# An RWKV-5 and mixture-of-experts kernel on one core: gate weights loaded as rows and turned on TensorE, with five smaller edits of order

## The chip, the cores and the metric

The kernel runs on one core of one Trainium2 chip. The metric is the device time of one execution in microseconds (us). Three runs of the kernel before gave a median of 400.97 us, between 399.18 and 401.94.

The engines are named as the profile names them: PE is TensorE (PEld its weight loads), DVE is VectorE, ACT is ScalarE, POOL is GpSimd, SP is SyncE, which here issues most DMAs.

## The reference

Two parts follow each other. The first is a linear recurrence per head with a decay `w` and a bonus `u`; the second sends each token to one of 16 experts. All numbers are fp32.

```python
# r, k, v: (4, 8, 768, 48); w, u: (8, 48)
for t in range(768):
    cur = k[t] outer v[t], each row times u
    y[t] = r[t] @ (state + cur)
    state = w * state + k[t] outer v[t]
x = y as (3072, 384)                   # tokens by (head, 48)
# experts: w_group (384, 4), w_expert (4, 384, 4), w1 (4, 4, 384, 1024), w2 (4, 4, 1024, 384)
g = argmax(x @ w_group)                # one group for each token
e = argmax(x @ w_expert[g])            # one expert in the group
gate = softmax(x @ w_group)[g] * softmax(x @ w_expert[g])[e]
out = gate * (relu(x @ w1[g, e]) @ w2[g, e])
```

## The kernel before, in words

The order of the work on every engine is written out by hand: each engine runs its instructions in the order in which the code issues them, and semaphores tie the engines together where a tile is shared.

**The recurrence.** The 3072 tokens are 24 tiles `n` of 128, four batches beside each other. One step `s` of the loop at L860 treats one tile. In a step, `values(s)` (L583) multiplies the masked scores `am` with `v` into `y_ps` in bank YB; `values_out(s)` (L612, ACT) copies the result to `yT`; `scores` (L536) makes the scores of a coming tile in bank PA, and `mask` (L543, DVE) writes those below the diagonal into `am`. On the diagonal stands the bonus term: POOL multiplies r, k and u (`own`, L489 and L490), DVE sums it (`sum_own`, L498), DVE writes five of the eight diagonals (`diagonal_here`, L554) and ACT the other three (`diagonal`, L561; they are kept in `waiting` and issued behind the next `values_out`). `update` (L594) makes the new part of the state in `u_ps`, in bank MS, which `carry` (L604, or L607 and L608 from tile 4 on, DVE) adds to the state R; `state` (L574) applies R. `turn` (L511) transposes k and r of a tile that comes later into the banks TR and RW; ACT copies k out (L520), DVE multiplies r by the powers of w on its way out (L522). POOL's `scaled` (L493) prepares k in the ring `kp`.

Up to `CLOSE = 5` a step makes the scores of tile s+1, and from then on those of tile s+2; step 4 turns one tile more than the others. Ahead of the loop, tiles 0 and 1 are prepared by the same helpers. Empty transposes of the identity (`turn_nothing`, L422) run in four places there: 13 at the start, 2, then 2 and 4.

**Routing.** `gate_parts(n)` (L619) multiplies yT with the gates' weights `gwp`, four quarters at once, into a bank (MS or TR, by the tile's number), and ACT copies the parts to `lT` (L624). `gate_sum` (L644) adds the quarters into the logits LG, also in MS. `rows_out` (L630, L634) turns y into rows of tokens. For four tiles at once the `route_` helpers on DVE find expert, gate and place; `route_5` (L230, POOL) scatters the rows of tokens to `x_sorted`, a DRAM tensor with a region for each expert. Four `fill` DMAs (L439) write zeros there first, in the steps 5 to 8.

`gwp` is filled by five DMAs (`gates_in`, L406 and L409), issued on SP behind the loads of the first three pairs of tiles. They read the weights in pieces of four numbers, since a partition of `gwp` holds one of a head's 48 dimensions. `gates_twice` (L412, POOL) copies a part of them to the partitions from 64 on.

In step 0 DVE compares w with its limited copy (`out_of_range`, L752), and PE and DVE make one flag of it (L756, L759); it decides at the very end whether a slow exact path runs.

**Experts.** From L1016 on the experts run one after another in the order of their numbers of tokens. Each has SLOTS[s] places for tokens; the two with most tokens are also computed ahead for 128 tokens each. `up` (L1104) and `down` (L1116) are the two products, `finish` transposes the result back and scatters it in pieces (L1128, POOL). The last to run is slot 0 with 96 places. Its `down` is done by `rows_down` (L240): tokens lie on the partitions of the result, ACT multiplies by the gate (L244), and one indirect DMA writes rows of 384 numbers (L245). `tokens` makes the row numbers `idA` for that.

Of the kernel before, what the change touches and what calls it, by code (L numbers as in the profile page):

```python
# [17 lines left out]
P = 128  # L18
# [11 lines left out]
def kernel(  # L30
# [89 lines left out]
    idA = [cst([P, 1], f"idA_{i}", I32) for i in range(4)]  # L120
    okA = [cst([P, 1], f"okA_{i}", I32) for i in range(4)]
# [130 lines left out]
    def tokens(i, n, count):  # L252
        nc.vector.memset(idA[i][0:n], NOWHERE)
        nc.vector.tensor_scalar(
            out=tagA[i][0:n, 0:1].bitcast(I32), in0=tagA[i][0:n, 0:1].bitcast(I32), scalar1=2, scalar2=None,
            op0=OP.logical_shift_right,
        )
        nc.vector.tensor_scalar(out=okA[i][0:n], in0=prow[0:n], scalar1=count[0:n], scalar2=None, op0=OP.is_lt)
        nc.vector.copy_predicated(idA[i][0:n], okA[i][0:n], tagA[i][0:n, 0:1].bitcast(I32))
# [14 lines left out]
    with ExitStack() as rec:  # L274
# [4 lines left out]
        lT_at = (MS[:, 0:P], TR[:, 0, :])  # L279

# [23 lines left out]
        cnt_ps = MS[:, 464 : 464 + GE]  # L304

# [25 lines left out]
        raw = {}  # L331
        wcol = ring.tile([P, HC], FP32, name="wcol")
# [17 lines left out]
        raw[0, "v"] = load(v, 0, "vt", 4)  # L350
        raw[1, "k"] = load(k, 1, "kt", 3)
# [52 lines left out]
        def gates_in():  # L404
            wg = moe_w_group.rearrange("(h d) g -> d h g", d=D)
            nc.sync.dma_start(out=gwp[0:D, :, 0:G], in_=wg)  # L406
            for g in range(G):
                we = moe_w_expert[g].rearrange("(h d) x -> d h x", d=D)
                nc.sync.dma_start(out=gwp[0:D, :, G + Eg * g : G + Eg * (g + 1)], in_=we)  # L409
# [10 lines left out]
        def turn_nothing(times, bank=RW):  # L420
            for i in range(times):
                nc.tensor.transpose(bank[:, 0, :], ident, ident)  # L422

        turn_nothing(13)
        nc.tensor.matmul(u_ps_all, lhsT=ones[0:1, :], rhs=u_row, start=True, stop=True, skip_group_check=True)
        turn_nothing(2)
        gates_in()
        pads(kp, 0)
        nc.scalar.copy(ub.rearrange("p h d -> p (h d)"), u_ps_all)
        for n in (1, 2, 3):  # L430
            if n < NRP - 1:
                pads(rp, n)
            pads(kp, n)
# [90 lines left out]
        def scores(n):  # L524
            kT, rT = rkT.pop((n, "kT")), rkT[n, "rT"]
            for hc in range(HC):
                for e in range(2):
                    rows = slice(DP * e, DP * e + D)
                    if n == 0:
                        nc.tensor.matmul(  # L530
                            PA[:, e, P * hc : P * (hc + 1)], lhsT=kT[rows, hc, :], rhs=rT[rows, hc, :],
                            start=True, stop=True, skip_group_check=True,
                        )
                        continue
# [79 lines left out]
        def gate_parts(n):  # L614
            yT = yTs[n]
            lT_ps = lT_at[n % 2 if n < 7 else 1]
            for q in range(NQ):
                e, j = q // 2, q % 2
                nc.tensor.matmul(  # L619
                    lT_ps[32 * q : 32 * (q + 1), :], lhsT=gwp[:, 4 * j + e, :], rhs=yT[:, e, j, :],  # L620
                    start=True, stop=True, skip_group_check=True,
                )
            lT = mid[n] = pool.tile([P, P], FP32, tag="lT", bufs=3, name="lT")
            nc.scalar.copy(lT, lT_ps)  # L624
# [60 lines left out]
        def count(n):  # L685
            nc.tensor.matmul(cnt_ps, lhsT=ones, rhs=cum[:, n, :], start=True, stop=True, skip_group_check=True)

# [63 lines left out]
        def out_of_range():  # L751
            nc.vector.tensor_tensor(out=same, in0=wcol, in1=wraw, op=OP.not_equal)  # L752
            nc.vector.reduce_max(out=same[:, 0:1], in_=same, axis=AX)

        def all_out_of_range():
            nc.tensor.matmul(cnt_ps[:, 0:1], lhsT=ones, rhs=same[:, 0:1], start=True, stop=True, skip_group_check=True)  # L756

        def in_range():
            nc.vector.tensor_scalar(out=not_ok, in0=cnt_ps[:, 0:1], scalar1=0.5, scalar2=None, op0=OP.is_gt)  # L759
# [68 lines left out]
        nc.vector.tensor_mul(WL, pw[:, :, P // 2], pw[:, :, P // 2])  # L828
        nc.scalar.copy(wl, WL)
# [3 lines left out]
        turn_nothing(2)  # L833
        turn(1, "rT")
        turn_nothing(4, TR)
        turn(1, "kT")
        scaled(1, 0)
# [22 lines left out]
        for s in range(NT):  # L860
# [11 lines left out]
            del left[0:some]  # L872
            if s == 2:
                gates_twice()
                late_consts()
# [19 lines left out]
            if s in (5, 6, 7, 8):  # L895
                fill(s - 5)
# [10 lines left out]
            values_out(s)  # L907
            if s == 0:
                own_term(1)
                out_of_range()  # L910
            for n, e, hc in waiting:
                diagonal(n, e, hc, hc + 1)
            waiting.clear()
            if s <= CLOSE:
# [13 lines left out]
            if s == 0:  # L928
                all_out_of_range()
                in_range()  # L930
# [11 lines left out]
            for n in {4: (0, 1), 5: (2, 3), 6: (4,), 7: (5, 6)}.get(s, (s - 1,) if s > 7 else ()):  # L942
                gate_sum(n)
            for c in range(NB - 1):
                if s == first(c) + 2:
                    route_p(c)
                    if c == 2:
                        count(12)
            for n in {3: (0, 1), 4: (2, 3), 5: (4,), 6: (5, 6)}.get(s, (s,) if s > 6 else ()):
                gate_parts(n)  # L950
            if s < CLOSE:
                own_term(far)
            for c in range(NB - 1):
# [4 lines left out]
                if s == first(c) + 2:  # L958
                    if c == 2:
                        key = keys()  # L960
                    route_3(c)
# [17 lines left out]
            if s + 1 < NT:  # L979
                state(s + 1)  # L980
            if s == CLOSE - 1:
                turn(s + 3, "kT")
# [6 lines left out]
            if s == 8:  # L989
# [450 lines left out]
```

## Time and profile before

| | us |
|---|---|
| median of three runs | 400.97 |
| profiled execution | 402.09 |
| its span in the profile | 400.3 |
| PE busy in the span | 388.7 |
| ACT / POOL / DVE busy | 180.4 / 201.0 / 153.4 |
| step 0's first values (L583) begin | 12.14 |
| PE's last matmul (L240) ends | 393.14 |

The profile is of one execution. A busy time counts an engine's instructions, not how full each of them uses it. A wait is named by what released it, as far as semaphores show; where the named engine had long been done, something else ended the wait. Times in the timeline count from the start of the span. Entries of the timeline merge like instructions in a row: start, length, engine, line, operation, tiles, count, and in brackets how long the engine was idle before and what ended that.

### The profile page before, as it was taken

To read this page: it belongs to the slowest core of one execution; us is meant where nothing else is said; L and a number is where in the kernel's file an instruction comes from. 1 tells how busy PE (TensorE), PEld (TensorE's weight loads), DVE (VectorE), ACT (ScalarE), POOL (GpSimd) and SP (SyncE) were. 2 spreads that over 40 slices of the span, in tenths; PEclk is the share of its full clock that TensorE was granted. 3 is DMA by queue.
4 is the path that set the end of the run, shared out by engine and by line. 5 is a ranking of instruction groups with operands and counts; after the bars stand their busy time and mean duration, and the time that the engine had idled before them with its cause. 6 is when DMAs were issued, how large, how long until landed. Compare 5 with 4: busy or idle time off the path is not lost.

```text
span 400.3 us, 10467 instructions
## 1 busy us (share of the span) xinstructions
PE 388.7 (97%) x3963; PEld 361.9 (90%) x3963; DVE 153.4 (38%) x405; ACT 180.4 (45%) x429; POOL 201.0 (50%) x265
## 2 busy tenths in 40 slices
PE   8999999999999999999999999999999999999992
PEld 6787899999888977899999999999999999999981
DVE  7887988888867602101202112111121221211110
ACT  4665888888875211432433424424244244244210
POOL 7999956999842412105162351532624524523542
PEclk9999999999999999999999999999999999999999
DMA  8998999995965977999999999999989999981000
GB/s 159 160 174 159 197 208 221 212 195 147 264 200 123 308 193 212 233 275 258 232 258 243 228 250 266 224 253 284 200 240 259 255 247 268 233 236 28 27 18 27
DMA packets 123118, 81.80 MB, mean 204 GB/s; under 512 B 96863, under 2 KB 114289, under 8 KB 123061
## 3 DMA queue, kind: packets, MB, share of 16 engines
q1 hardware_dynamic: 116019, 71.12, 77.1%
q0 software_dynamic: 4752, 9.55, 8.1%
q8 instruction: 32, 0.52, 0.6%
q10 hardware_dynamic: 2290, 0.40, 0.5%
q14 instruction: 25, 0.20, 0.2%
HBM read 69.89 MB, written 11.67 MB: 204 GB/s over the span
## 4 chain that ended last, share of the span: by engine, by line
issue 46%; PE 29%; POOL 18%; SPq 3%; DVE 2%; DMA 1%; POOLq 1%; ACT 0%
POOL out_dram L1128 16%; PE YB L583 6%; PE PA L536 6%; SPq L323 3%; PE TR L511 3%; PE YB L574 2%; PE YB L630 2%; PE RW L511 2%; PE MS L594 2%; PE TR L619 2%; PE MS L644 1%; DMA vt<-in_v_dram 1%; POOL out_dram L245 1%; PE TR L793 1%; DVE am L543 1%
## 5 line engine op out<-in xcount | busy, mean ns | idle before, releaser
L1128 POOL DMA_INDIRECT out_dram<-yt,idn x93 | 90.4, 972 | 137.1 <-DVE yt L1126 107.0
L1076 DVE STREAM_TRANSPOSE xe<-xg 128x672 f32<-128x672 f32 (+2 forms) x16 | 12.7, 796 | 121.0 <-DMA xg<-x_sorted 88.7
L1116 PE MATMUL YB<-hT,w2p 128*128 128x208 f32 (+10 forms) x336 | 58.7, 328 | 0.0
L1116 PE MATMUL PA<-hT,w2p 128*128 128x208 f32 (+10 forms) x336 | 58.1, 326 | 0.0
L1116 PEld LDWEIGHTS YB<-hT,w2p 128*128 128x128 f32 x336 | 55.8, 190 | 0.0
L1116 PEld LDWEIGHTS PA<-hT,w2p 128*128 128x128 f32 x336 | 55.3, 190 | 0.0
L561 ACT ACTIVATE am<-ident,du 128x128 f32<-128x128 f32 x152 | 50.5, 398 | 0.0
L1125 DVE STREAM_TRANSPOSE yt<-yT 128x672 f32<-128x672 f32 (+1 forms) x14 | 11.8, 842 | 80.4 <-ACT yT L1119 80.4
L1094 ACT COPY w2p<-w 128x1024 f32<-128x1024 f32 x42 | 41.1, 1045 | 3.0 <-DMA w<-in_moe_w_dram 3.0
L543 DVE COPY_PREDICATED am<-later,PA 128x1024 f32<-128x1024 int32 x24 | 31.7, 1323 | 10.8 <-PE PA L536 6.1
L1104 PE MATMUL MS<-xe,w 128*128 128x208 f32 (+12 forms) x192 | 32.8, 320 | 0.0
L1104 PE MATMUL TR<-xe,w 128*128 128x208 f32 (+12 forms) x192 | 32.8, 320 | 0.0
L1104 PE MATMUL RW<-xe,w 128*128 128x208 f32 (+12 forms) x192 | 32.8, 320 | 0.0
L1104 PE MATMUL SB<-xe,w 128*128 128x208 f32 (+12 forms) x192 | 32.7, 320 | 0.0
L1104 PEld LDWEIGHTS SB<-xe,w 128*128 128x128 f32 x192 | 30.8, 190 | 0.6 <-issue 0.2
L1104 PEld LDWEIGHTS MS<-xe,w 128*128 128x128 f32 x192 | 30.7, 190 | 0.0
L1104 PEld LDWEIGHTS RW<-xe,w 128*128 128x128 f32 x192 | 30.7, 190 | 0.0
L1104 PEld LDWEIGHTS TR<-xe,w 128*128 128x128 f32 x192 | 30.7, 190 | 0.0
L230 POOL DMA_INDIRECT x_sorted<-xt,place_i x16 | 16.1, 1003 | 23.6 <-DVE end L719 11.8
L536 PE MATMUL PA<-rT,kT 48*64 48x128 f32 (+1 forms) x736 | 25.6, 255 | 0.5 <-issue 0.5
L583 PE MATMUL YB<-am,vt 128*48 128x128 f32 x384 | 25.9, 277 | 0.1
L490 POOL TENSOR_TENSOR dg<-dg,ub 128x384 f32<-128x384 f32 x24 | 24.1, 1003 | 1.9
(220 smaller groups left out, 560.1 us busy)
## 6 DMA issues: line engine op xcount, KB each, us to landing
w<-in_moe_w_dram SPq DMA_DIRECT2D x128, 384.0 KB, 9.5
vt<-in_v_dram SPq DMA_DIRECT2D x24, 192.0 KB, 4.5
rp<-in_r_dram SPq DMA_DIRECT2D x23, 192.0 KB, 4.3
kt<-in_k_dram SPq DMA_DIRECT2D x22, 192.0 KB, 5.2
xg<-x_sorted SPq DMA_DIRECT2D x36, 85.8 KB, 10.3
x_sorted<-zeros SPq DMA_DIRECT2D x4, 392.0 KB, 4.7
out_dram<-yt,idn POOLq DMA_INDIRECT x93, 7.5
xg<-x_sorted SPq DMA_DIRECT2D x20, 73.5 KB, 8.9
```

Source lines behind the costliest of these rows:

```text
L230: ins = nc.gpsimd.indirect_dma_start(out=xs_dram, out_offset=bass.IndirectOffsetOnAxis(ap=place_i[:, i : i + 1], axis=0), in_=xt[:, i].rea ...
L490: nc.gpsimd.tensor_mul(dg, dg, ub)
L511: nc.tensor.transpose(ps[:, hc, :], two, ident)
L536: nc.tensor.matmul(PA[64 * z : 64 * (z + 1), e, P * hc + 64 * z : P * (hc + 1)], lhsT=kT[rows, hc, 64 * z : 64 * (z + 1)], rhs=rT[rows, hc ...
L543: nc.vector.copy_predicated(am[n % NAM], later.unsqueeze(1).unsqueeze(1).to_broadcast([P, 2, HC, P]).bitcast(I32), PA.rearrange("p e (h t) ...
L561: nc.scalar.mul(am[n % NAM][:, e, hc, :], ident, dus[n][:, i : i + 1])
L583: nc.tensor.matmul(y_at(e, hc), lhsT=vt[:, n % 2, 2 * hc + e, :], rhs=amn[:, e, hc, :], start=(n < 4 and hc < 2), stop=True, skip_group_ch ...
L1076: nc.vector.transpose(xe[:, :, 0:nb, :], xg[:, 0:nb, 0:QW].rearrange("p i (ko a) -> p ko i a", a=32))
L1094: nc.scalar.copy(o4[:, kk], v4[:, kk])
L1104: nc.tensor.matmul(ph[:, i, 0:n], lhsT=w1[:, ko, P * (f + i) : P * (f + i + 1)], rhs=xe[:, ko].rearrange("p i b -> p (i b)")[:, 0:n], star ...
L1116: nc.tensor.matmul(po[:, 0:n], lhsT=w2p[:, d, fo, :], rhs=hT[:, fo, 0:n], start=(fo == 0), stop=(fo == FO - 1))
L1128: ins = nc.gpsimd.indirect_dma_start(out=out_q, out_offset=bass.IndirectOffsetOnAxis(ap=idn[:, i : i + 1].bitcast(U32), axis=0), in_=yt[:, ...
```

## The change

It has six parts.

1. **Gates' weights.** Two DMAs load them as 32 rows and 8 rows of 768 bytes, each row a head of a group, into the ring tile `kp[3]`, which is not in use yet; they are issued ahead of `raw[1, "k"]`. Four transposes (`gates_turned`) turn them into bank MS behind the turns of tile 1, and two ACT copies write `gwp`. The pads of `kp[3]` are written in step 1.
2. **Head.** The 13 empty transposes write over bank PA instead of one spot of RW; the other eight are gone. The scores of tile 0 are made in quarters like all others. WL and its copy come behind the mask of tile 0. The range check moves from step 0 to step 8; its sum shares a matmul with `count` in step 14.
3. **Zero fill.** The last fill is issued in step 7 instead of step 8.
4. **Gate parts** of two tiles lie side by side in TR and are copied by one ACT instruction. Before step 5, parts and sums come behind `state` instead of ahead of it.
5. **Step 4.** `values_out` comes behind the diagonals, and the additional turn of k goes to PA instead of TR.
6. **Last product.** `half_down` makes the last expert's result in two halves of 192 columns, each with its own multiply and its own indirect DMA of rows of 192 numbers. `tokens` makes two sets of row numbers for that.

```diff
-    def tokens(i, n, count):
+    def half_down(hT, w2, i, n, z, po, yt):
+        cols = slice(DM // 2 * z, DM // 2 * (z + 1))
+        for fo in range(FO):
+            nc.tensor.matmul(po[0:n, 0 : DM // 2], lhsT=hT[:, fo, 0:n], rhs=w2[:, fo, cols], ...
+        nc.scalar.mul(yt[0:n], po[0:n, 0 : DM // 2], tagA[i][0:n, 1:2])
+        ins = nc.gpsimd.indirect_dma_start(
+            out=out.rearrange("n (z w) -> (n z) w", z=2),
+            out_offset=bass.IndirectOffsetOnAxis(ap=idH[z][0:n].bitcast(U32), axis=0),
...
+    def tokens(i, n, count, halves=False):
...
-        lT_at = (MS[:, 0:P], TR[:, 0, :])
+        lost_ps = MS[:, 464 + GE : 464 + GE + 1]
...
+        gates = kp[3].rearrange("p a h x -> p (a h x)")[0 : H * G + H, 0 : D * Eg].rearrange("p (d x) -> p d x", x=Eg)
+        def gates_in():
+            nc.sync.dma_start(out=gates[0 : H * G].rearrange("p d x -> p (d x)"),
+                in_=moe_w_expert.rearrange("g (h d) x -> (g h) (d x)", d=D))
+            nc.sync.dma_start(out=gates[H * G :].rearrange("p d x -> p (d x)"),
+                in_=moe_w_group.rearrange("(h d) x -> h (d x)", d=D))
...
         raw[0, "v"] = load(v, 0, "vt", 4)
+        gates_in()
         raw[1, "k"] = load(k, 1, "kt", 3)
...
-        def gates_in():
-            wg = moe_w_group.rearrange("(h d) g -> d h g", d=D)
-            nc.sync.dma_start(out=gwp[0:D, :, 0:G], in_=wg)
-            for g in range(G):
-                we = moe_w_expert[g].rearrange("(h d) x -> d h x", d=D)
-                nc.sync.dma_start(out=gwp[0:D, :, G + Eg * g : G + Eg * (g + 1)], in_=we)
+        def gates_turned():
+            n = H * G + H
+            ps = MS.rearrange("p (x c) -> p x c", c=P)
+            for x in range(Eg):
+                nc.tensor.transpose(ps[0:D, x, 0:n], gates[:, :, x], ident[0:n, 0:n])
+            nc.scalar.copy(gwp[0:D, :, G : G + GE] ..., ps[0:D, :, 0 : H * G] ...)
+            nc.scalar.copy(gwp[0:D, :, 0:G] ..., ps[0:D, :, H * G : n])
...
-        turn_nothing(13)
+        for i in range(13):
+            nc.tensor.transpose(PA[:, i // 4 % 2, P * (i % 4) : P * (i % 4 + 1)], ident, ident)
         nc.tensor.matmul(u_ps_all, ...)
-        turn_nothing(2)
-        gates_in()
...
-                    if n == 0:
-                        nc.tensor.matmul(PA[:, e, P * hc : P * (hc + 1)], lhsT=kT[rows, hc, :], rhs=rT[rows, hc, :], ...
-                        continue
                     for z in range(2):
...
-        def gate_parts(n):
-            lT_ps = lT_at[n % 2 if n < 7 else 1]
+        def gate_parts(some):
+            for i, n in enumerate(some):
+                for q in range(NQ):
+                    nc.tensor.matmul(TR[32 * q : 32 * (q + 1), i, :], ...
+            m = len(some)
+            lT = pool.tile([P, m, P], FP32, tag=f"lT{m}", bufs=3 - m, name="lT")
+            nc.scalar.copy(lT, TR[:, 0:m, :])
...
-        nc.vector.tensor_mul(WL, pw[:, :, P // 2], pw[:, :, P // 2])
-        nc.scalar.copy(wl, WL)
         for t in am[2:4]:
             nc.scalar.copy(...)
         mask(0)
-        turn_nothing(2)
+        nc.vector.tensor_mul(WL, pw[:, :, P // 2], pw[:, :, P // 2])
+        nc.scalar.copy(wl, WL)
         turn(1, "rT")
-        turn_nothing(4, TR)
         turn(1, "kT")
+        gates_turned()
...
+            if s == 1:
+                pads(kp, 3)
...
-            if s in (5, 6, 7, 8):
-                fill(s - 5)
+            for i in {5: (0,), 6: (1,), 7: (2, 3)}.get(s, ()):
+                fill(i)
...
-            values_out(s)
+            if s != CLOSE - 1:
+                values_out(s)
             if s == 0:
                 own_term(1)
-                out_of_range()
             for n, e, hc in waiting:
                 diagonal(n, e, hc, hc + 1)
             waiting.clear()
+            if s == CLOSE - 1:
+                values_out(s)
...
-            if s == 0:
-                all_out_of_range()
-                in_range()
...
+            if s >= CLOSE:
+                gate_parts(parts)
+            if s == CLOSE:
+                for n in summed:
+                    gate_sum(n)
...
                 state(s + 1)
+            if s < CLOSE:
+                for n in summed:
+                    gate_sum(n)
+                if parts:
+                    gate_parts(parts)
             if s == CLOSE - 1:
-                turn(s + 3, "kT")
+                turn(s + 3, "kT", PA[:, 0].rearrange("p (h t) -> p h t", t=P))
...
             if s == 8:
+                out_of_range()
+            if s == 17:
                 go_on()
...
+                if p == last:
+                    for z in range(2):
+                        yt = pool.tile([P, DM // 2], FP32, tag="yh", name="yh")
+                        half_down(hTs[p], held(p)[1], 2 + i, SLOTS[i], z, next_of(downs), yt)
```

## The prediction

> **What bounds the kernel now.** First the page's busy times, then the stretches of the span, then the timeline where TensorE (PE) is not full.
>
> ```profile
> PE 388.7 (97%) x3963; PEld 361.9 (90%) x3963; DVE 153.4 (38%) x405; ACT 180.4 (45%) x429; POOL 201.0 (50%) x265
> ```
>
> PE is idle for 400.3 - 388.7 = 11.6 us. The stretches say where (columns: length, busy us of PE, PEld, DVE, ACT, POOL):
>
> ```profile
> 25.00:30.00 5.00, 4.73 (x97) 3.91 (x100) 4.41 (x8) 2.97 (x8) 4.70 (x8) 1.00 0.95 180
> 30.00:38.00 8.00, 7.47 (x140) 6.04 (x142) 5.10 (x9) 3.88 (x12) 7.54 (x14) 1.00 0.90 167
> ...
> 63.00:68.00 5.00, 5.00 (x108) 4.64 (x104) 4.53 (x15) 4.37 (x14) 4.66 (x5) 1.00 1.02 223
> ```
>
> From step 5 on PE is full to 393 us, but for about 1.1 us near 103 and 110 us. An edit there pays only if it takes work off PE, and this change takes almost none. What can be won lies in three places: before step 1, in steps 3 to 5, and behind the last product. A gain made early is kept, since after it the chain runs through PE and the expert weights are asked for only when the routing is known.
>
> The head, from the timeline of the first 22 us:
>
> ```profile
> 5.96 0.69 PE L422 MATMUL RW<-ident 128*128 128x128 f32 x2
> 6.45 1.06 PE L511 MATMUL MS<-ident,rp 128*128 128x128 f32 x4
> 7.30 1.06 PE L808 MATMUL TR<-ident,rp 128*128 128x128 f32 x4
> 8.40 0.69 DVE L810 TENSOR_TENSOR kT<-TR,iw 128x512 f32<-128x512 f32 x1
> 9.23 1.16 PE L530 MATMUL PA<-rT,kT 48*128 48x128 f32 x16
> ...
> 13.29 0.59 ACT L612 COPY yT<-YB 128x512 f32<-128x512 f32 x1 [0.52 <-PE YB L583]
> 13.78 0.98 ACT L561 ACTIVATE am<-ident,du 128x128 f32<-128x128 f32 x3
> 14.33 0.49 DVE L752 TENSOR_TENSOR same<-wcol,wraw 128x4 f32<-128x4 f32 x1
> 14.93 1.32 DVE L543 COPY_PREDICATED am<-later,PA 128x1024 f32<-128x1024 int32 x1
> 16.55 0.38 PE L756 MATMUL MS<-same,ones 128*128 128x1 f32 x2 [0.60 <-DMA vt<-in_v_dram]
> 16.86 1.08 PE L583 MATMUL YB<-am,vt 128*48 128x128 f32 x16
> ```
>
> Two empty transposes (L422) stand right ahead of the first real ones; in step 0 the range check (L752, L756) stands ahead of mask and values of step 1.
>
> Steps 3 and 4, from the timeline of 22 to 45 us:
>
> ```profile
> 29.34 0.43 PE L619 MATMUL MS<-yT,gwp 128*32 128x128 f32 x8 [0.27 <-issue]
> ...
> 32.11 0.99 ACT L561 ACTIVATE am<-ident,du 128x128 f32<-128x128 f32 x3
> 33.13 1.33 DVE L543 COPY_PREDICATED am<-later,PA 128x1024 f32<-128x1024 int32 x1 [1.91 <-PE MS L594]
> 34.84 0.59 PE L644 MATMUL MS<-sel,lT 128*128 128x20 f32 x4 [0.27 <-DVE ts L607]
> 36.84 0.63 PE L511 MATMUL TR<-ident,kp 128*128 128x128 f32 x4 [0.25 <-ACT lT L624]
> ```
>
> PE waits three times: for bank MS (read by the carry, L604 and L607) and for TR (emptied by the second lT copy). The end:
>
> ```profile
> 393.18 0.58 ACT L244 ACTIVATE yd<-YB,tagA 96x384 f32<-96x384 f32 x1 [4.83 <-PE YB L240]
> 394.03 0.94 POOL L245 DMA_INDIRECT out_dram<-yd,idA  x1 [1.76 <-ACTq L1170]
> ```
>
> **What the Trainium skill says.** "TensorE: Matmul & The Clock Gate", Part 1: the array starts at half clock and goes to full after about 3.4 us of activity. The trace agrees in effect: weight loads of transposes take 230 ns until 8.8 us and 140 ns from 10.5 us, while the PEclk column reads 1.00 throughout. "DMA: Bandwidth & Descriptors", Specifications: transfers under 512 bytes miss line rate. Here the five gate loads (16-byte pieces, 48 x 8 for each) keep the DMA engines 0.51 busy from 18 to 21 us at 15 to 24 GB/s. "ScalarE: Activation LUTs", What ACT_TABLE_LOAD costs: 0.833 ns per element and column on a fixed part; the trace's 96x384 multiply (580 ns) then becomes about 420 ns at 192 columns, an estimate from that page.
>
> **The change, part by part.**
>
> *Empty transposes.* In the half clock four transposes take 7.30 - 6.45 = 0.85 us, so two cost 0.43. The r rows were issued at 1.39 us and land within 4.9 us, pw is done at 6.42, iw at 6.82, all before they are needed. So transposes, kT (8.40 to 7.97), first scores, T2 and with it POOL's chain all come 0.43 earlier. The six fillers at 10.3 and 10.9 us stand in time in which PE waits for the mask: nothing. Scores in quarters: twice the instructions at half the width; the quartered form (L536) takes 1.10 us beside the 1.16 of L530, and diagonals and mask hide either. If they fall into the half clock, they lose up to 0.3, or gain 0.1.
>
> *Mask of step 0.* WL (0.34) and wl leave the way; the mask then waits for ACT's three diagonals instead (10.61 - 0.43 = 10.2). It ends near 11.6 instead of 12.08, and values(0) begins at 11.65 instead of 12.14.
>
> *Gates' weights.* Out go five loads of 2.7 us on SP's queue (16.77 to 19.55), which moves the loads of step 0 forward by as much; nothing waited for them. In come two loads of 32 and 8 rows ahead of raw[1,"k"], about 0.4 us each by the row of tagA (0.36). They carry 31 KB, at 200 GB/s 0.15 us of DMA, and delay the loads behind them by 0.2 to 0.8 us. POOL's first use behind them is own(1) at 14.75; SP issued its rows at 7.64 and they land within 4.9, so 2.2 us of slack cover it. Four small transposes take PE at most 0.5 us while it waits for the mask. Two ACT copies of 48x128 and 48x32 cost 0.27 and 0.22 by L624 (128x128) and L639 (128x16). These are *not* hidden: ACT goes kT(1), the two copies, yT(0), three diagonals, and the mask of step 1 waits for those. With kT(1) done at 12.6, the copies end at 13.1, yT at 13.7, the diagonals at 14.7. Bounds: 0.3 (short copies) to 0.8 (a strided output slow); I take 0.5. The pads of kp[3] move to step 1, where ACT idles 1.88 us ahead of yT.
>
> *Range check.* L752 and L753 (0.65 of DVE) and the matmul that waits for the carry leave step 0. The mask of step 1 now begins at 14.7, limited by ACT, and ends at 16.0; values(1) begins at 16.1 instead of 16.86. With the 0.43 above this makes **0.8 us**. The check returns in step 8 behind sum_own: 0.65 us of DVE, which has about 0.7 us idle in a 4.8 us step, and whose masks from step 5 on are made two steps ahead. Count and range share a matmul of 17 columns instead of 16: nothing.
>
> *Steps 1 and 2* go on at 4.06 us: values, yT, diagonals, mask, and PE is full beside that.
>
> *Step 3.* state(4) goes ahead of the gate parts and needs neither MS nor TR; the gate parts find TR emptied at 29.31. The 0.27 goes.
>
> *Step 4.* With yT(4) behind the diagonals, these no longer wait for values: they end near 31.7, so the mask waits only for scores(5) and moves from 33.13 to 32.45 on the old clock (0.68, of which 0.27 is already counted). PE now runs without a gap: values 1.03, scores 1.03, update 0.52, rows 0.60, two turns 0.87, state 0.58, sums 0.26, parts 0.65, two turns 0.87 = 6.4 us, from 30.3 to 36.7, where the old step ended at 37.91. So steps 3 and 4 win 1.2. The turn into PA needs the mask's reading done (33.8) and stands at 35.8; its copy is out before scores(6).
>
> *Step 5.* The gate parts go to TR, the sums behind them find the carry done; the old 0.19 wait goes and the mask, held by DVE's chain, follows: 0.25. Together **1.45 us** in steps 3 to 5. One lT copy for two saves ACT about 0.15, hidden.
>
> *Zero fill.* The last piece lands before the loads of step 8 instead of behind them. POOL stood still from 55.42 to 63.07 ahead of its first scatter, which writes where the fill writes; it will resume about 6 us earlier. PE never waited for it, so nothing; the loads of step 8 come up to 2 us later, which POOL's slack covers.
>
> *Last product.* PE: 32 matmuls of 192 columns for 16 of 384, the same 5.3 us. The first half's multiply and scatter lie under the second's matmuls and behind the 13th group's last scatter (ends 392.27). Then multiply 0.42 for 0.58 (-0.16), the scatter 0.94 as before, half the bytes behind it: 0 to -0.4. I take **0.4 us**.
>
> **Sum**: 0.8 + 1.45 + 0.4 = 2.65 us off the profiled execution, 402.09 (span 400.3 and 1.8 around it), gives 399.4. That execution lies 1.1 above the median 400.97, so 398.3.
>
> **Rivals.**
>
> *Small gain.* Head and step 0 are lost: cold scores (0.3), slower copies on ACT (0.3), late loads. For it: DVE, ACT and POOL are all near full there. Against: every wait was followed. 2.65 - 1.0: 399.3.
>
> *Large gain.* The PE gaps near 103 and 110 us fall together with bursts of early expert weights (309 to 348 GB/s); POOL's memsets release these, and an earlier POOL spreads them. If the 1.1 us go as well and the tail gives its 0.6: 396.9. Against: the trace does not name what PE waits for.
>
> *Slower.* The turned gates stand in PE's order ahead of values(0). If the two small loads queue behind 1.2 MB of r, k and v, PE stops. They are issued near 5.1 us and needed at 11.1, and 0.55 us of slack follow the estimate for values(0). It eats all gains from a landing at about 14.3 us, 9.2 after issue; at 10.4 after issue the kernel takes 402.2. For it: weights later land 9.5 us after issue (median). Against: r, k, v in the head land 3.2 to 5.7 after issue.
>
> **How the numbers follow.** Likeliest 0.62, at 398.3 (397.0 to 399.5); small gain 0.17 at 399.3; large 0.16 at 396.9; slower 0.05 at 402.2. The range 396.2 to 400.6 takes in the bounds of copies, cold scores and tail. One per cent is 4.0 us, about what a measurement can tell here: faster by more needs under 397.0, that is half of the large case and the low edge of the likeliest, 0.17; slower by more needs a landing beyond 17 us, 0.03; the rest 0.80.
>
> **What would show it.** Right: the first real transposes near 6.0; values(1) near 16.1; values of step 5 near 35.9 (37.84 less 2.0); no PE wait on MS or TR in steps 3 to 5; POOL's first scatter near 56; PE's end near 390.9; a last multiply of 0.42. Wrong: gates' transposes that wait for a DMA; a mask(1) behind 15; new PE gaps after 45 us; or, at the end, a PE whose early gain has been given back in the experts, where the loads now share their bounds with it.

## The result and the profile after

The changed kernel takes 398.56 us (median of 22 runs, 397.36 to 401.29); the kernel before, run beside it, 401.15 (22 runs, 399.17 to 404.06). The ratio is 0.9945, 95% interval 0.9929 to 0.9961: 2.2 us less (2.6 between the medians), with 398.3 forecast. The profiled execution fell from 402.09 to 398.76, its span from 400.26 to 397.04.

```profile
PE 387.6 (98%) x3989; PEld 363.6 (92%) x3989; DVE 154.2 (39%) x408; ACT 180.5 (45%) x429; POOL 202.6 (51%) x266
```

PE's busy time shrank by 1.1 us of the span's 3.2; the rest is idle time that went. Line numbers in a fence are those of its own kernel. The stretches of steps 3 and 4 (columns as before: length, busy PE, PEld, DVE, ACT, POOL, PE clock, DMA share, GB/s) are full now, where PE stood 0.27 and 0.53 us idle:

```profile
25.00:30.00 5.00, 5.00 (x110) 4.04 (x108) 4.43 (x8) 2.81 (x8) 4.70 (x7) 1.00 0.93 163
30.00:38.00 8.00, 8.00 (x162) 6.66 (x158) 6.08 (x10) 3.94 (x12) 7.52 (x14) 1.00 0.94 164
```

The head, the first values of step 5 and the end, from the timeline of the changed kernel:

```profile
5.97 1.11 PE L545 MATMUL MS<-ident,rp 128*128 128x128 f32 x4
8.81 1.75 PE L564 MATMUL PA<-rT,kT 48*64 48x128 f32 x32
10.68 1.35 DVE L571 COPY_PREDICATED am<-later,PA 128x1024 f32<-128x1024 int32 x1 [0.40 <-PE PA L564]
...
13.05 0.39 ACT L443 COPY gwp<-MS 48x128 f32<-48x128 f32 x1
13.22 0.27 ACT L447 COPY gwp<-MS 48x32 f32<-48x32 f32 x1
14.84 1.35 DVE L571 COPY_PREDICATED am<-later,PA 128x1024 f32<-128x1024 int32 x1 [0.31 <-PE MS L622]
16.25 1.08 PE L611 MATMUL YB<-am,vt 128*48 128x128 f32 x16 [0.41 <-DVE am L571]
...
36.32 1.08 PE L611 MATMUL YB<-am,vt 128*48 128x128 f32 x16
...
390.38 0.42 ACT L260 ACTIVATE yh<-PA,tagA 96x192 f32<-96x192 f32 x1 [2.18 <-PE PA L256]
```

The gain can be followed by the start of each step's values, before less after, in these two profiles and in a second pair (`again_before` less `again_after`):

| values of step | 0 | 1 | 3 | 4 | 5 | 6 | 17 | 18 | 19 | 23 | first expert | PE's end |
|---|---|---|---|---|---|---|---|---|---|---|---|---|
| gained, us | 0.05 | 0.61 | 0.57 | 0.91 | 1.52 | 1.77 | 1.77 | 2.57 | 3.63 | 3.63 | 2.91 | 2.79 |
| second pair | 0.07 | 0.63 | 0.57 | 0.92 | 1.53 | 1.79 | 1.56 | 2.63 | 3.68 | 3.68 | 3.31 | 3.04 |

The span won 3.22: 2.79 to PE's end, 0.43 behind it. The total came out as forecast, but from other places than the prediction's sum: nothing in the head, 1.7 us up to step 6, and another 1.86 in steps 17 and 18, where two waits of PE are gone, with 0.7 given back where the experts begin (0.4 in the second pair).

The kernels below are compared with runs of the kernel before in the same group, whose median was 400.8 to 401.2. Medians count all runs, but ratios leave out runs that lie well above the others (three of the 14 of `fill_only`), and one whole group was slow: the kernel before itself took 436.4 there, so the totals of `head_old`, `pad_before` and `gates_act` mean nothing, and only what lies ahead of 70 us is read from them (with notes on two of them at `pad_before`).

### The profile page after: what moved, and what is told of

Its sections match the earlier page's. It is cut to its first block, busy times and chain, and to the rows that moved or that the text cites. A ratio compares the mean times of both kernels' runs of the same rounds, so it can differ in the third digit from the quotient of the medians.

```text
span 397.0 us, 10511 instructions
## 1 busy us (share of the span) xinstructions
PE 387.6 (98%) x3989; PEld 363.6 (92%) x3989; DVE 154.2 (39%) x408; ACT 180.5 (45%) x429; POOL 202.6 (51%) x266
## 4 chain that ended last, share of the span: by engine, by line
issue 46%; PE 32%; POOL 18%; DVE 2%; POOLq 1%; ACT 0%; DVEq 0%
POOL out_dram L1175 16%; PE PA L564 6%; PE YB L611 6%; PE TR L545 3%; PE YB L602 3%; PE YB L660 2%; PE RW L545 2%; PE TR L646 2%; PE MS L622 2%; PE MS L674 1%; PE PA L459 1%; PE TR L826 1%; DVE am L571 1%; PE RW L660 1%; POOL out_dram L246 1%
## 5 line engine op out<-in xcount | busy, mean ns | idle before, releaser
L571 DVE COPY_PREDICATED am<-later,PA 128x1024 f32<-128x1024 int32 x24 | 32.5, 1354 | 9.6 <-PE PA L564 7.5
L564 PE MATMUL PA<-rT,kT 48*64 48x64 f32 (+1 forms) x768 | 27.0, 259 | 0.1
L564 PEld LDWEIGHTS PA<-rT,kT 48*64 48x64 f32 x768 | 21.2, 135 | 4.8 <-issue 4.1
L231 POOL DMA_INDIRECT x_sorted<-xt,place_i x16 | 16.1, 1006 | 18.4 <-DVE caps L764 11.7
```

The source lines that it names most:

```text
L231: ins = nc.gpsimd.indirect_dma_start(out=xs_dram, out_offset=bass.IndirectOffsetOnAxis(ap=place_i[:, i : i + 1], axis=0), in_=xt[:, i].rea ...
L564: nc.tensor.matmul(PA[64 * z : 64 * (z + 1), e, P * hc + 64 * z : P * (hc + 1)], lhsT=kT[rows, hc, 64 * z : 64 * (z + 1)], rhs=rT[rows, hc ...
L571: nc.vector.copy_predicated(am[n % NAM], later.unsqueeze(1).unsqueeze(1).to_broadcast([P, 2, HC, P]).bitcast(I32), PA.rearrange("p e (h t) ...
```

## The experiments

The theory after the result: PE is the bound, but POOL and SP's loads stand close behind it, so a part that makes PE earlier pays only as far as other parts make POOL and the loads earlier too. The rival is the prediction's own view: every part has its price, and prices add.

**Both kernels again.**

> The kernel before, profiled a second time, to see which stage times repeat. Theory A (mid-stage gaps are chance): values of steps 1, 5 and 6 begin within 0.1 us of 16.86, 37.84 and 44.46, but the two PE gaps of 0.50 us near 103 and 0.64 us near 110 sit elsewhere or are missing. Theory B (the late zero fill and POOL behind it cause them): they come back within 1 us of their places and at about the same length.

> The changed kernel, profiled a second time. Theory A: values of steps 1, 5 and 6 begin within 0.1 us of 16.25, 36.32 and 42.69, and gaps of half a microsecond on PE may turn up between 95 and 115 us. Theory B: no gap there again, and from step 6 to step 23 the values come 81.0 us apart as in the first profile (42.69 to 123.73), against 82.9 us in the kernel before (44.46 to 127.36). For the head: if the phase of the clock gate is chance, the last slow weight load is not at 9.9 us again.

Measured: 402.37 and 398.72, one run each. Stage times repeat: values of step 6 at 42.69 in both profiles of the changed kernel, last PE product ends at 390.35 and 390.39. The two waits of PE near 103 and 110 us stand again in `again_before` (0.76 and 0.64) and are missing in `again_after`; they belong to the kernels. The late fill does not cause them, as `fill8` and `fill_only` show below.

**The zero fill put back to step 8.**

```diff
-            for i in {5: (0,), 6: (1,), 7: (2, 3)}.get(s, ()):
+            for i in {5: (0,), 6: (1,), 7: (2,), 8: (3,)}.get(s, ()):
```

> The changed kernel with the last zero fill back in step 8. Theory A: POOL's first scatter moves from 58.3 back to about 62 us, PE's stages stay within 0.3 us of the changed kernel's, ratio to the kernel before 0.994 to 0.996 as with the change. Theory B: PE gaps of 1 to 2 us return between 95 and 115 us, values of steps 6 to 23 are 82 to 83 us apart, and the time is 1 to 1.9 us above the changed kernel's, ratio 0.997 to 0.999.

Measured: 401.89 (14 runs), ratio 1.0009 (0.9987 to 1.0031). An edit priced at nothing takes the whole gain with it, and the loss is larger than either expectation had it. From the timeline of this kernel, POOL's first scatter and a PE wait that neither kernel had:

```profile
65.85 1.20 POOL L231 DMA_INDIRECT x_sorted<-xt,place_i  x1 [9.02 <-DMA kt<-in_k_dram]
136.28 1.91 PE L826 MATMUL PA<-xeA,w 128*128 128x128 f32 x15 [2.22 <-DMA w<-in_moe_w_dram]
```

SP issued the last fill at 60.60, and such a fill lands 3.7 to 6.2 us later, so the scatter stood behind the fill, whatever the bracket names; in all five profiles with this fill in step 8 the scatter begins 5.2 to 5.5 us after the fill's issue. It ran at 58.28 in the changed kernel. POOL stayed late: its one-column memsets that release the early expert weights (L737) ran from 92.55 on instead of 86.94, the last ones at 116.69 instead of 112.42; SP issued the last early weights at 129.75 instead of 124.26; PE came to them at 134.06 and stood. In the kernel before the last fill was issued at 57.60, since SP's queue runs 2 to 3 us earlier there, the last early weights at 127.05, and PE came to them at 136.40 and never met them. So in the changed kernel the early expert weights are a deadline just behind PE. PE also waited 0.50 for POOL's keys at 70.19. The waits between 95 and 115 us, which the second expectation named, did not come back, though POOL was late.

**The fill alone, steps 3 to 5 alone, and both, each on the kernel before.** `fill_only` is the edit above the other way round. `steps345_only` has this core:

```diff
+            if s == CLOSE - 1:
+                values_out(s)              # behind the diagonals
...
-            for n in {3: (0, 1), 4: (2, 3), ...}.get(s, ...):
-                gate_parts(n)              # ahead of state
+            if s < CLOSE:                  # behind state
+                for n in summed: gate_sum(n)
+                if parts: gate_parts(parts)
...
-                turn(s + 3, "kT")
+                turn(s + 3, "kT", PA[:, 0].rearrange("p (h t) -> p h t", t=P))
```

> The kernel before with one edit: the last piece of the zero fill in step 7, beside the third, instead of in step 8. Prediction's view (the fill is worth nothing, PE never waits for it): 401.1, ratio 1.000, stages of PE as before. Theory now (POOL's first scatter writes where the fill writes; POOL sets when the early expert weights are asked for; PE meets them only if it is early): POOL's first scatter near 56 to 58 us instead of 62 to 63, the early weights' loads 2 to 4 us earlier, PE's stage times up to 95 us unchanged; ratio 0.997 to 1.000, because PE is not early and the weights came in time before. If the fill carries the whole gain by itself, through the two PE gaps near 103 and 110 us: these gaps go, and the ratio is 0.996 or less.

> The kernel before with the reordering of steps 3 to 5 alone (gate parts in pairs behind the state, values of step 4 copied behind the diagonals, one turn of step 4 into another bank). Prediction: 1.45 us. By the stages of the changed kernel: values of step 6 begin 1.2 us earlier (43.3 instead of 44.46). Theory that early expert weights stand just behind PE: the gain is given back, in a PE wait for weights near 134 us or in the gaps near 103 and 110 us, total 400.5 to 401.5, ratio 0.999 to 1.002. Rival (a gain in PE is kept): last PE product ends 1.2 us earlier, total 399.9, ratio 0.997.

> The kernel before with both edits, the reordering of steps 3 to 5 and the fill's last piece in step 7. Theory (the fill moves the early weights ahead, so an early PE finds them): 1.2 us and more are kept, last PE product ends at 391.5 to 392, total 399.3 to 399.9, ratio 0.995 to 0.997, no PE wait for weights near 134 us. Rival (the two edits add nothing to each other): the sum of the two ratios measured beside it, 0.997 to 1.000.

| on the kernel before | median us, runs | ratio | values of step 6 | POOL's first scatter | PE's end (profile) |
|---|---|---|---|---|---|
| nothing | 400.82, 62 | | 44.46 | 63.07 | 393.14 |
| fill | 401.28, 14 | 1.0000 (0.9978 to 1.0022) | 44.42 | 59.44 | 394.31 |
| steps 3 to 5 | 400.34, 22 | 0.9991 (0.9973 to 1.0009) | 43.27 | 61.75 | 392.13 |
| both | 399.67, 22 | 0.9985 (0.9973 to 0.9997) | 42.80 | 57.82 | 390.83 |

Alone the fill moves POOL by 3.6 us and the time by nothing; up to step 17 PE's stages stay within 0.1 us. PE is not early enough to profit, as the theory had it. But the profile shows something else as well: with POOL earlier, the first of PE's two waits stands at the same product, and is longer:

```profile
105.27 0.44 PE L536 MATMUL PA<-rT,kT 48*64 48x128 f32 x9 [1.99 <-issue]
```

The reordering wins 1.19 in its stages, as expected; alone its total isn't told from no change. In its profile, though, 1.0 us of this is kept to PE's end, with no wait for weights near 134 us: in it the rival is right, and the theory that an earlier PE gives its gain back is not. Both together are just told from it (0.1 to 1.1 us), less than the 0.995 to 0.997 that the theory had named and within what the rival allows for a sum. Their profile cannot be put beside the others for the head: there the clock had risen early (below), and values of step 0 begin at 11.68 instead of 12.14. So these three show what the fill does and do not prove that the two help each other; that rests on `fill8`.

**The range check back in step 0** (on the changed kernel).

```diff
             if s == 0:
                 own_term(1)
+                out_of_range()
...
+            if s == 0:
+                nc.tensor.matmul(lost_ps, lhsT=ones, rhs=cum[:, 13, 0:1], ...)
+                in_range()
```

> The changed kernel with the range check back in step 0, its two instructions on DVE and its product on PE ahead of the mask and the values of step 1. Prediction's step: the check costs 0.65 us of DVE ahead of mask(1), so with it values of step 1 begin at 16.8 to 16.9 instead of 16.25 us, and each later stage up to the last PE product is 0.5 to 0.6 later. Rival (mask(1) is set by ACT's diagonals, which the gates' copies made late, so the check would have been hidden): values of step 1 at 16.3 to 16.5. Total 398.6 to 399.3, ratio 0.993 to 0.996.

Measured: 399.61 (15 runs), ratio 0.9976 (0.9962 to 0.9989), about 1.2 us of the gain, twice what was expected. From its timeline:

```profile
15.46 1.35 DVE L571 COPY_PREDICATED am<-later,PA 128x1024 f32<-128x1024 int32 x1
17.10 0.38 PE L966 MATMUL MS<-cum,ones 128*128 128x1 f32 x2 [1.28 <-DVE R L632]
```

The mask of step 1 begins 0.62 later (15.46 for 14.84), the price of L752 and L753 in the prediction: not hidden by ACT. The other half is the product: here it shares bank MS and waits until the carry (L632), behind the mask, has read it. Values of step 1 begin at 17.41 instead of 16.25. The kernel before had the second half too: its product used the same bank and stood 0.60 us, and values of step 1 began 0.61 behind the end of the mask (16.25, 16.86), with 0.06 in the changed kernel.

**The gates' weights as before** (five loads of 16-byte pieces, no transposes, no two copies; on the changed kernel).

```diff
-        gates_in()                     # ahead of raw[1, "k"]: two loads of rows
...
+        gates_in()                     # behind the product of u: five loads, as before
...
-        gates_turned()
```

> The changed kernel with the gates' weights loaded as before: five loads of 16-byte pieces on SP's queue behind the first rows, no transposes and no two copies on ACT. All else as in the changed kernel. Prediction's term: the two copies cost 0.5 us on ACT ahead of the diagonals of step 1, and nothing waited for the five old loads; so values of step 1 begin at 15.8 to 16.0 instead of 16.25 us, later stages up to the last PE product are 0.3 to 0.4 earlier, total 398.2, ratio 0.9935: the first part of the change would be a small loss. Rival (the five loads, 2.8 us of issue on SP in step 0, push the rows of later steps past POOL's need, and PE stops): values of step 1 near 15.9, but a PE wait between 20 and 32 us, values of step 4 at 29.6 or later, ratio 0.995 to 0.998.

Measured: 400.16 (22 runs), ratio 0.9985 (0.9967 to 1.0003), about 1.6 us of the gain: the rival's total. Values of step 1 begin at 16.06, but those of step 0 had begun 0.17 earlier as well (11.92 for 12.09), so on the path the two copies cost next to nothing, and not 0.5. But then, in SP's queue, POOL and PE:

```profile
25.55 1.44 SPq L345 DMA_DIRECT2D rp<-in_r_dram  x2
...
30.55 1.00 POOL L508 TENSOR_TENSOR dg<-rp,kt 128x384 f32<-128x384 f32 x1 [2.68 <-DVE am L567]
...
40.56 1.11 PE L530 MATMUL TR<-ident,kp 128*128 128x128 f32 x4 [1.78 <-POOL kp L512]
```

The five loads hold SP from 18.82 to 21.52, and these rows of r are issued at 25.55 instead of 23.14. POOL, which needs them, stands 2.68, until 5 us after their issue (the bracket names another engine), and PE stands 1.78 for POOL's keys, at 38.8 and not between 20 and 32 us as the rival had it. Values of step 6 begin at 45.94 instead of 42.69. This profile is of an execution of 403.42, the upper end of its runs, so the usual wait is probably smaller. "Nothing waited for them" was true of the kernel before, with PE later and the rows of r issued at 22.54.

**The gates' two loads issued by ACT** (on the changed kernel).

```diff
         def gates_in():
-            nc.sync.dma_start(...)
+            nc.scalar.dma_start(...)       # both loads
```

> The changed kernel with the two loads of the gates' weights issued by ACT instead of SP, behind the activation that loads ACT's table. Theory (the 2.99 us of the first load on SP are back-pressure of SP's own queue, filled by the r, k and v loads ahead of it): about 0.4 to 0.8 us for each on ACT, raw rows of step 1 issued on SP at 5.0 to 5.5 us instead of 8.36, POOL's wait of 0.8 us near 20 us gone, values of step 0 within 0.2 of 12.09, last PE product unchanged within 0.3. Rival (it is the price of this load's shape, whichever engine issues it): 3 us on ACT, the copy of u and the pads 1.5 us later, and values of step 0 at 12.4 to 13. Total 398.3 to 399, ratio 0.993 to 0.996, or 0.996 to 0.999 in the rival.

From the queues of ACT and SP in this kernel:

```profile
3.14 1.28 ACTq L357 DMA_DIRECT2D kp<-in_moe_w_expert_dram  x1
4.99 0.37 ACTq L361 DMA_DIRECT2D kp<-in_moe_w_group_dram  x1
...
5.05 4.26 SPq L345 DMA_DIRECT2D kt<-in_k_dram  x2
9.36 2.07 SPq L345 DMA_DIRECT2D rp<-in_r_dram  x2
```

On SP the first of these loads took 2.99 us (4.91 to 7.90), on ACT 1.28: not a price of its shape, though above the 0.4 to 0.8 that was expected. But the rows behind gain nothing. r of step 1 is issued at 9.36, with 9.42 in the changed kernel; now k takes 4.26 where the load of the gates had stood. Without the gates' loads SP was done with k at 9.31, with them at 9.37. Our reading is that SP issues there as fast as its transfers drain, so that whoever stands in its queue waits. POOL's wait for r near 20 us shrinks from 0.79 to 0.54, values of step 0 begin at 12.05 (12.09).

**The head as before** (on the changed kernel).

```diff
+        for i in range(2):                 # behind the product of u
+            nc.tensor.transpose(RW[:, 0, :], ident, ident)
...
+                    if n == 0:             # scores of tile 0 in one piece
+                        nc.tensor.matmul(PA[:, e, P * hc : P * (hc + 1)], ...)
+                        continue
```

> The changed kernel with the head of the kernel before: two empty transposes again ahead of the first real ones, and the first scores in one piece of 128 columns. Prediction's step: the two transposes cost 0.43 us, so without the removal values of step 0 begin near 12.5 us instead of 12.09, the last PE product ends 0.4 later, total 399.0, ratio 0.9955. Theory now (the array is still in half clock when the quartered scores run, and they lose there what the transposes gave): first scores at 9.23 instead of 8.81, but over sooner; values of step 0 at 12.1 to 12.2, total 398.6, ratio as that of the changed kernel, 0.993 to 0.996.

Values of step 0 began at 11.80, earlier than the 12.09 of the changed kernel, though two transposes were added: neither expectation. One reason is in the timeline (`steps345_fill`, then `head_old`):

```profile
4.39 0.91 PE L424 MATMUL PA<-zeros,ones 1*128 1x384 f32 x2
```

```profile
6.58 0.66 PE L849 MATMUL TR<-ident,rp 128*128 128x128 f32 x4 [0.38 <-DMA rp<-in_k_dram]
```

In these two executions the product of u takes 0.91 and 1.00 us and four transposes 0.60 to 0.66; in the other profiles 1.64 and 1.00 to 1.12. The array rose to full clock between 4.4 and 5.2 us here and between 8.4 and 10.1 us in the others. "TensorE: Matmul & The Clock Gate", Part 1, says that the window which counts activity runs free, so that the number of cold products varies from run to run. It varies here too, but by 3 to 6 us, where the page gives half a microsecond; the measurement decides.

The other reason is on POOL. The kernel before, then `fill8`, which has the head of the changed kernel:

```profile
6.37 1.00 POOL L489 TENSOR_TENSOR dg<-rp,rp 128x384 f32<-128x384 f32 x1
```

```profile
6.82 1.00 POOL L523 TENSOR_TENSOR dg<-rp,rp 128x384 f32<-128x384 f32 x1 [0.40 <-DMA rp<-in_k_dram]
10.55 1.35 DVE L571 COPY_PREDICATED am<-later,PA 128x1024 f32<-128x1024 int32 x1
```

Removing the transposes brought the first scores from 9.23 to 8.81. In the profile of the changed kernel they then ran at half clock, 1.75 us instead of 1.16, and the mask waited for them until 10.68. In `fill8` they took 1.10, and the mask still began at 10.55, because the diagonals were done only at 10.51. The diagonals follow POOL's bonus term, whose first product begins at 6.37 in all six kernels built on the one before and at 6.68 to 6.99 in all eight built on the changed one; seven of these profiles name the rows of k as what it waited for. In `head_old` the scores were done at 9.33 and the mask began at 10.40. So two chains end at the mask, and the change moved that of the diagonals, done at 10.61 in the kernel before, by 0.2 at most: the term is near zero. The start of the clock moves the head by 0.3 to 0.5 from run to run.

**The last product whole** (on the changed kernel).

```diff
-                if p == last:
-                    for z in range(2): half_down(...)
-                else: ...
+                yt = pool.tile([P, DM], FP32, tag="yd", bufs=2, name="yd")
+                rows_down(hTs[p], held(p)[1], 2 + i, SLOTS[i], next_of(downs), yt)
```

> The changed kernel with the last product whole again (384 columns, one multiply, one scatter). From PE's last matmul to the end of the span: 7.1 us (as before) instead of 6.7; all earlier stages as in the changed kernel. Time 0.4 us above the changed kernel. Rival: the end is bound by the receipt of the last write alone, and 6.7 us stay.

Measured: 398.53 (6 runs), ratio 0.9931 (0.9905 to 0.9956), which overlaps with that of the changed kernel: the total can't resolve this part. The stage says more: from the end of PE to the end of the span 7.06 us, with 6.69 and 6.61 for the halves, and a last multiply of 0.58 for 0.42. That is 0.4. Single profiles scatter, though. Leaving out the group of `pad_before`, six with the whole product have 6.75 to 7.12 (mean 6.93) and five with the halves 6.37 to 6.69 (mean 6.56), so 0.4 holds for the means.

**33 more matmuls ahead of everything** (on the kernel before).

```diff
-        turn_nothing(13)
+        turn_nothing(6)
+        for i in range(20):
+            nc.tensor.matmul(RW[0:1, 0, 0:1], lhsT=ident[:, 0:1], rhs=ident[:, 0:1], ...)
```

> The kernel before with the 13 empty transposes of the head replaced by 6 and 20 products of one column, which adds 33 matmuls to PE's stream ahead of everything (66 instructions of the 256 that a 16 KB block of instructions holds) and changes nothing else. Theory (the PE gaps near 103 and 110 us are late blocks of PE's own instructions: in each profile the gap ends about 1.5 us behind a block that began 8 to 10 us after the one ahead): the gaps leave the two instructions at which all profiles of before have them; each lies 33 matmuls (about 2 us) earlier in the program or is gone, and where one stands, a block stands ahead of it with such a distance. Rival (those instructions wait for something that the profile does not show, a buffer or a semaphore): both gaps stay at the same scores and the same state product of step 17 and 18. Total 399.5 to 402; head up to 0.5 later or earlier.

This is about the two waits near 103 and 110 us, the 1.86 us of the table. The profile gives them no releaser. Timeline of the kernel before, then of `steps345_only`:

```profile
103.83 0.44 PE L536 MATMUL PA<-rT,kT 48*64 48x128 f32 x9 [0.50 <-issue]
110.69 0.43 PE L574 MATMUL YB<-rT,R 48*48 48x128 f32 x6 [0.64 <-issue]
```

```profile
102.77 0.44 PE L535 MATMUL PA<-rT,kT 48*64 48x128 f32 x9 [0.64 <-issue]
109.63 0.43 PE L573 MATMUL YB<-rT,R 48*48 48x128 f32 x6 [0.64 <-issue]
```

POOL's time alone is not the cause: `fill_only` has POOL early and keeps both waits, `fill8` has it late and has neither. What is left is the position in PE's stream. The queue of instruction transfers, from the DMA view of 91.5 to 100.5 us of the changed kernel (packets, MB, share of 16 engines):

```profile
q8 instruction: 1, 0.02, 0.8%
```

For the kernel before, the same view of the same stretch has no line for q8. More facts point the same way. Counted through all of PE's instructions in the trace (weight loads, products, semaphores), 3777 lie ahead of the first wait and 4033 ahead of the second in four profiles (both of the kernel before, `fill_only`, `steps345_only`), exactly 256 apart. `steps345_fill` has the first wait alone, at the same count; `head_old`, with another program, has one at 3777; and `range0` has one at 4289, the next step of 256, at other work:

```profile
114.45 0.71 PE L611 MATMUL YB<-am,vt 128*48 128x128 f32 x9 [0.44 <-issue]
```

q8 moves 32 or 33 packets of 16 KB in a run, one for some 250 of PE's instructions. Each of these 11 waits ends 2.4 to 3.2 us after a packet began that came late: 9.5 to 11.7 us behind the one before it at the first wait (in the kernel before at 91.1, then 100.9, with PE going on at 103.83), 7.3 to 7.4 at the second, 8.8 in `range0`; in the changed kernel the packets of this stretch stand 6.3 to 6.6 us apart. Lateness alone does not make a wait: in `fill8` and `again_after` packets of this stretch came 8.2 to 8.4 us behind the last, and PE did not stand. In `pad_before` neither of the two instructions has a wait, which speaks against something tied to them; but neither count has one either, so the move by 33 products that the theory forecast was not seen. So most likely these are late blocks of PE's own instructions; what makes a packet late stays open. That the change wins here would then be a matter of position: its 26 more matmuls move other work to these counts. This is argued, not tried.

No version beat the changed kernel beyond its interval; the whole last product (0.9931) cannot be told from it.

## Why the prediction was right, and where its steps were not

**Right in size and in mechanism.** *Range check*: 0.62 us of DVE as priced, values of step 1 at 16.25 where 16.1 was forecast; step 0 and the check together gave 0.61 of the 0.8, all but 0.05 of it in step 1. *Steps 3 to 5*: PE waits on neither MS nor TR, and `steps345_only` wins 1.19 alone; 1.16 in the changed kernel, of 1.45. The missing 0.3 is in step 4: its mask moved by 0.7 as the prediction had it, but PE's work there took 6.73 us (29.59 to 36.32) and not 6.4. The sum had the gates' sums at 0.26, where its own line shows 0.59 for the same four products and 0.55 was measured, and the four turns at 1.74, where 1.99 was measured. *Last product*: 0.4, by the means of the stage (0.43 in the profile). *PE's end*: 390.35, forecast 390.9. Two signs came short: values of step 5 began at 36.32 where 35.9 was forecast, and POOL's first scatter at 58.28 where 56 was.

**"So transposes, kT (8.40 to 7.97), first scores, T2 and with it POOL's chain all come 0.43 earlier."** The transposes, kT, the first scores and T2 did. But POOL's bonus term began 0.31 later (6.68 for 6.37), so the diagonals, for which the mask was to wait from now on, were done at 10.38 and not at 10.2 (10.51 in `fill8`). Of 0.49 for step 0 remained 0.05. The lower bound of cold scores (0.3) was named, then left out of the sum; the rows of k, for which POOL stood, were not looked at. The line on r holds an error too: issued at 1.39 and up to 4.9 under way makes 6.3, which is not ahead of transposes at 5.96. No profile shows a wait for r there, so it cost nothing.

**"PE never waited for it, so nothing."** Wrong, and the failure with most to teach. The fill was priced by the wait it removes, in a kernel where PE was late. With PE 2 to 3 us earlier the same fill decides 2.6 us (0.0064 of 401, `fill8` against the change). The same failure sits in the five gate loads (2.8 us from 16.77 to 19.55, not 2.7): "nothing waited for them", yet 1.6 us hang on them in the changed kernel (`gates_old`). Undone one by one, fill, gates and check cost 2.6 + 1.6 + 1.2 = 5.4 us, each to within about 1, and more than twice the whole gain; done alone, fill and reordering give 0 and at most 1.1. So the prices of these parts do not add.

**Gates' weights.** "About 0.4 us each" on SP was 2.99 and 0.37; `gates_act` shows that the queue, and not the load, was the limit, so the loads behind lost little. The two ACT copies (0.39 and 0.27, overlapping) cost next to nothing on the path, below the 0.3 of the bounds: the copy to yT behind them began at 13.29, as in the kernel before. The sign of the slower case, gates' transposes that wait for a DMA, showed in two kernels, 0.13 us in `range0` and 0.67 in `head_old`, both hidden behind the mask. Of the old loads, "0.51 busy from 18 to 21 us at 15 to 24 GB/s" holds from 19 us on (0.54 and 0.42); from 18 to 19 the DMA engines moved 116 GB/s.

**What the large case counted on came, but not by its mechanism.** The two waits vanished, worth 1.86 at that point and not 1.1. (Counted from product to product, PE stood 0.77 and 0.91 us there in the kernel before; the rest was not traced.) An earlier POOL that spreads the bursts of weights is not enough to explain it: with the fill alone POOL was 3.6 us earlier and the first wait grew to 1.99. 0.7 went back where the experts begin, as the last sentence of the prediction had it. In the changed kernel:

```profile
149.25 0.98 PE L1151 MATMUL SB<-xe,w 128*128 128x88 f32 x7 [0.56 <-PE TR L241]
```

The product can't begin before DVE has turned the expert's rows (148.67 to 149.15), which landed 5 us after their issue at 143.69; the kernel before had these rows 1.3 us ahead of PE. How much goes back changes from run to run: 0.4 in the second pair, and no such wait in `tail_whole`, which is the same kernel up to there. So against the sum of 2.65, up to step 6 1.77 came where 2.25 were due; then 1.86 from the two waits, less 0.72 at the first expert and 0.12 up to PE's end, and 0.43 behind it: 3.22 between the two profiled executions, 2.6 between the medians. That the forecast total was met is luck: the two waits, which were not in the sum, made up for the head and for what the experts took back.

## What to carry to other kernels

Price an edit off the critical path by the slack of the next deadline after all other edits have moved the bound, not by who waits for it today; then test it by undoing it from the finished kernel, since doing it alone on the old one can show nothing, as with the fill. Where a total can't resolve a part, compare the start of the same step in two profiles, and only between executions whose clock rose at the same time. Waits without a releaser that repeat at the same instruction, a fixed number of instructions apart, are worth a look at the queue of instruction transfers.

## What the runs showed of the hardware that was not expected

- PE began work at 1.43 us. Its full clock began between 4.4 and 5.2 us in 2 of 14 profiles and between 8.4 and 10.1 us in the others, with nearly the same head; the PEclk row of the page shows nothing of it.
- Instruction packets of 16 KB, one for some 250 of PE's instructions, run over the same DMA engines as the data. In 11 cases, at three counts of PE's instructions 256 apart, PE stood idle for 0.4 to 2.0 us, until 2.4 to 3.2 us after the start of a packet that came 7.3 to 11.7 us behind the last.
- Between 4.5 and 7 us the DMA engines moved 255 to 259 GB/s in all six kernels built on the one before, and 165 to 180 in all eight built on the changed one, with equal packets of 192 bytes (median 15 and 24 to 28 ns each). It doesn't come from the gate loads (`gates_old` 167) nor from the empty transposes (`head_old` 170). The cause was not found. POOL's first product, which reads rows of k, began 0.3 to 0.6 us later in these eight.
- The same DMA took SP 2.99 us to issue and ACT 1.28, and a smaller one behind it 0.37 on either.
